# Attention with chunk selection, then a wave mixer: scores of two heads on halves of the TensorE array, the mask as a second product

## The chip, the cores and the metric

The kernel runs on one NeuronCore of a Trainium2 chip. The metric is the device time of one execution in microseconds (us). Three runs before the change took 250.59, 250.40 and 251.05 us, median 250.59. The profiled execution has a span of 250.7 us, from its first to its last instruction, with a mean granted TensorE clock of 0.986. All durations below come from that one execution.

## What is computed

The inputs q, k and v have 4 batches, 8 heads, 768 positions and 64 values a head (fp32). Keys fall into 24 chunks of 32. For every query a bound of its score against each chunk is formed from the chunk's minimum and maximum, the six best chunks that are not in the future are kept, and ordinary causal attention runs over the kept chunks alone:

```python
k_min, k_max = k_chunks.min(axis=3), k_chunks.max(axis=3)
ub = np.sum(np.maximum(q[..., None, :] * k_min, q[..., None, :] * k_max), axis=-1)
ub = np.where(causal, ub, -1e9)
top_chunks = np.argsort(ub, axis=-1)[..., -6:]
scores = np.where(sel & (pos[:, None] >= pos[None, :]), scale * q @ k.T, -1e9)
attn_out = softmax(scores) @ v
```

The 8 heads are put side by side to x (768 x 512 for each batch), and a mixer follows:

```python
theta = x @ w_theta
y = w_tok_r @ (x * cos(theta)) + w_tok_i @ (x * sin(theta))
u = x + y
out = u + np.maximum(u @ w_ch, 0)
```

## The kernel before, in words

The program is recorded first and emitted afterwards. `record` makes a list of operations. Each has a name, the engine (or several engines) that may run it, what it reads and what it writes. The long text `ORDER` gives the order of emission by the operations' numbers. A letter b or c behind a number takes the second or third engine of the choice. `F10` stands for ten filling products of 128 columns (L637), which keep TensorE (PE) busy and compute nothing. Ten more of 512 columns stand at the start (L633). Each engine runs its own instructions strictly in this order, so `ORDER` settles what stands behind what. `CLASSES` (L100) says how many buffers of each kind there are; `decode` (L654) hands them out in the order of use, and a buffer that is used again waits for its last reader.

For every batch b and every pair p of heads, `pair` (L188) does the following:

- It loads k and q of the two heads side by side (L174) and v (L182), all on SP's queue.
- It turns k and q with fp32 transposes on PE, three blocks at a time (L197), into `kps` and `qps`. Afterwards head 0 has partitions 0 to 63 and head 1 has 64 to 127.
- It copies k to `kx` and q to `qx` in fp16, each head by itself, to partitions 0 to 63 (L164 on ACT, L166 on DVE, L167 on POOL are the three choices of one copying helper). For the first two pairs of batch 0 (`direct`) k goes by way of an fp32 copy `kT`.
- It takes minimum and maximum over each chunk on DVE (L221, to `km`) and their difference (L226), and makes relu(q) as `qr` (L248 on DVE or POOL, L250 on ACT).

`group` (L258) makes the selection, in general for two pairs at once. The bounds `ub` are fp32 products of 64 rows by 32 columns (L280), placed by head on rows 0 or 64 of the array and by pair and run of queries on four column groups. Then DVE transposes them (L295), overwrites what lies in the future with a large negative value (L303), takes the eight largest of each query (L308), marks the chunks that fall below the sixth (L312) and transposes the marks to `nsT` (L317). From there the marks are copied into rows 64 to 87 of `qx`, by head, pair and run (L325). Rows 64 to 87 of the five `kx` buffers hold a one-hot of the key's chunk times -1000, loaded once by `Loh` (L531). Queries below 192 have at most six chunks and need no selection.

`head` (L335) forms one head's scores, transposed, so that keys are on partitions. One product over 88 rows (64 of k and q, 24 of one-hot and marks) gives score plus mask (L357). A head has three steps, each two key blocks: 1024, 1024 and 640 columns of PSUM, in two `sc` buffers of two banks each. In batch 0 the triangle on the diagonal is added by another product (L361). In the other batches it is cut after the exponential, on POOL (L377) or DVE (L375). ACT takes the exponential of a step to `pt` (L367). The weighted values `av` are 21 products of 65 columns with `pt` as weights (L398); the 65th column is the sum, by which DVE divides (L408, L409) into `x16`.

`mixer` (L413) turns x (L427), multiplies by w_theta (th, L437), takes sine and cosine on ACT (L444, L448), forms the products zr and zi (L452), multiplies by the turned token weights (y, L462 and L464), adds x (L470), turns the sum (ups, L478) and multiplies by w_ch (ch, L486); then come L492 and the store. PSUM buffers of class `mi` (three) serve all transposes, bounds and mixer products; `av` has one buffer.

Work of different batches overlaps: the list puts the next batch's pairs, selection and scores between the mixer products of the batch before.

Of the kernel before, what the change touches and what calls it, by code (L numbers as in the profile page):

```python
# [1 line left out]

# [8 lines left out]
FP16 = mybir.dt.float16  # L11
# [6 lines left out]
    "6 0 8 5 51 50 7 52 53 31 97 98 15 4 9 16 10 96 20 18 F10 54 12 13 60 11 14 55 95 26 61 17 19 22 56 27 64 "  # L18
    "76 23 62 58 30c 29 121 59 F19 67 28 24b 65 71 25 122 68b 72 57 70b 21 63c 75c F16 33 66 32 73b 120 34 69b "
    "74 42 F9 78 35 162 43 112 36 44 113 119 37 3 F11 110 45 87 111 117 46 38 F10 99 116c 49c 88 104 115 79 1 "  # L20
    "48b 100 89 41c 39b 108 47b 114 107 F17 228 226 101b 77 141 105 102 106 40c 227 103 406 90 F15 136 80 109b "
    "134 229 91 407 218 81 137 216 135b 219 168 163 217 F5 214 2 82 139c 123 140c 83 138 128 426 126 224 215 "
    "166 130b 86c 85c 132 125 222 84 221 94b 131 118 225 236 127 220 124b 164 133b 237 234 93 92 223 143 142b "
    "231 235 144 230 404 244 153 405 145 232 129 154 248 146 245 419 169 421 233 249 246 429 147 422 155 294 "
    "196 247 238 428 148 156 152b 427c 252 239 250 251 157 151c 184 295b 167 420b 276 253 160c 423b 278 193 "
    "425b 241 277 158 240 159 242 424 408 243 279 413 165 274 410 181 417 296 150c 161b 178 409b 275 264 412 "
    "197 411 265 284 416 198 437 285 418b 282 280 441 185 286 430 440 414 288 431 287 194c 281 187 283 202 438 "
    "266 195 289 182c 267 292 291 211 290 268 439 186 293 149b 179 432 269 254 434b 415 180 256 436 255 271 "
    "435 445 433b 257 272 442b 450 258 199 443 259 270 183 273 444 446 300 190 297b 260 448c 262 261 188 301b "
    "263 449b 447b 189 298 452 299 203 471 302 453 472 462 496 307 212c 304 463 495 454 312 464 455 451 309 "  # L30
    "213 308 306 311 313 322 310b 314 465 456 303 204 466 315 317 323 457 324 327 305b 208 318 468 461 474 470 "
    "332 459 319 467 316 333 328 473 458 339 321 329 469 544 325b 580 460c 545 480 331 340 330 484 341 483 334 "
    "482b 320 581 538 481b 475 539 191 342 479 497 557 326b 192 476b 335 558 577 478 582 541 477 174 540b 343 "
    "578 485 559 498 504 209c 344 542 508 546 205 551 579 345 210 336 200 506 549 488 552 507 543 583 337 201 "
    "489b 584 548 553 505b 547 499 338 585 486 172 501 550 564 176 487 175 554 170 500 586 491 492c 587 493 "
    "502 510 555 503 512 490 588 511b 753 346 513 509b 589 752 347 556 206b 567 516b 562 514b 754 560 515 519 "
    "207 568 561 529 348 565 520 569 349 530 521 350 531 755 177b 566 353 173b 522 374 517 354 171b 774 355 "
    "532 375b 523 778 356 533 357 524 537b 534c 358 563 494 526b 386 779 359 528c 570 536 776 527 642 525 571 "
    "535 635 387 351 777 643b 572 609 352 761 610 573 388 574 765 636 378 611 762b 603 379b 575 764 637 596 "
    "604 767 576 392 768b 763 605 606 597 393 644 607 769 598 394 645 590 822 518c 756 770 821 593 608 591 759 "  # L40
    "380 775 613 760 612 771b 376 381 798 632 592 757 766 395 772c 846 758 377b 793 396 594 614 841 389 615 "
    "773c 397 595 791 601 794 600 865 792 599 390 780 633 797b 785 845 783 622 360 788 796b 391 634 619 789 "
    "781 361 602 1102 787 362 623 782b 363 1103 364 784 786 624 620 365 795c 834 790b 366 629 799 835 367 630 "
    "621 800 1126 1127 368 631 801 640 810 638 639 802 842 382 811 803 616 646 617 641 1122 369 370 804 647b "
    "371 812 618 372 866b 805 626 813 836 809b 808 625 819 814 806c 627 837 915 807c 1169 383 816b 858 818 820 "
    "840c 628 817c 892 838 1170 398 916 859b 839 373 648 893 889 399 917 384 890 894 886 649 400 815c 860 385 "
    "655 887 861b 844 843 891b 670 863c 657 888 862 902 650 864b 656 905 659 897 672 1123 895 660 652 674 1101 "
    "896 658b 651 1100 654 662 665 653b 898 671 661 675 673b 667 664 663 680 666 681 676 401 668b 677 669 903 "
    "678 682 402 823 683 403 679 684 827 685 826 828 906 904 686 899 1125 825 912 832 1124 824 852 907b 900 "
    "831 687 688 855 833b 830 689 856 901 829 931 853 908 847 854 690 849 1168 1104 932 1167 848b 910 691 1105 "  # L50
    "850 925 1106 851 692 913 1108 909 694 693 926 695 933b 696 1107 1109 911 927 722 1110 1146 697 723 928 "
    "1112 990 1113 929 698 991 699 1114 1111b 918 930 734 700 919 914b 935 857 735 920 934 867 1147c 736 936 "
    "701 1193 877 868 702 1194 878 1117 869 879 724 1118 703 725b 870 704 1115 880 1141 871 1116 1189 705 881 "
    "1142 1121b 706 872 1120b 1133 937 883c 708 873b 882c 709 874b 1137 875c 876b 951 707 1134 944 1135 884 "
    "922 885 945 921 1136 923 710 952 924 946 957 1190 711 958 992 953b 954 1213 993 1119b 959 938 712 955 713 "
    "1128 939 714 956 962 941 1192 1132 960 1191 961 942 940 1131 967 963 726 1138b 1130 1139 943 970 1129 "
    "1140b 949 727b 948 947 1145 971 1184 1144 950 1148 1185 1143b 1214c 740 1158 972 968 1149 980 741 1182 "
    "981 969 983 1159 1150 742 737 1160 984 1151 964 1183 985 977 965 738 1188b 1176 715 739 1161 1187b 716 "
    "1179 966 975 1186 1162 974 978 973 1180 728 1166c 717 976 729b 979 718 1177 1165 719 1152 1178 1163 720 "
    "1153 730 1164 1157b 1154c 721 1171 731b 1253 1155c 1174 1250 1156c 1254 746 1175 1251 1172b 1234 1181 747 "  # L60
    "1173 1195 1237 1235 1252b 748 1199 743 982b 1198 1238 1240 1236b 986 744 988 1241 987 1239b 1260 745 989 "
    "1197 1247 1196 1208 1242b 1261 1255b 1244 1209b 1243 1245 1200 1248 1262 1246 1266 732 1206 1204 1267 "
    "1273 733 1207 1258 1268 1203 1279 1274 749 1212b 1202b 1210c 1201 994 750 1205b 1280 1276 996 1249b 1211b "
    "751 1281b 1263 997 1257 1277 1275b 1256 995 1215 1259 1264 998 1216 1278b 1271 1217 1008 1000 1265b 1218 "
    "1270 1225 1269 1219 1003 1272 1009 1220 1010 1282 1011 1283 1226 999 1284 1227 1023 1004 1001b 1005 1223 "
    "1013 1002 1024 1221 1007 1018 1025 1006b 1026b 1014 1027 1042 1019 1224 1043 1016b 1015 1285 1315 1312 "
    "1020 1021b 1340 1012 1313 1063 1228 1341 1017b 1064 1229 1065 1056 1232 1230 1066 1222 1022b 1316 1057 "
    "1058 1314b 1292 1317 1286 1293 1233c 1067 1231c 1287 1068 1294b 1299 1069 1044 1288 1300 1305 1045 1306 "
    "1046 1301 1047 1307 1302 1048 1289 1303 1049 1050 1290 1304b 1310 1318 1309 1319 1308 1291b 1051 1311 "
    "1052 1035 1320b 1322 1321 1323 1331 1324 1036 1332 1037 1295 1333b 1296 1297 1038 1298 1039 1040 1053 "  # L70
    "1041 1325 1054 1326 1342 1055 1328 1059 1343 1329 1060 1327b 1061 1330b 1076 1062 1072 1335 1073b 1336 "
    "1077 1334 1338 1337 1085 1339 1344 1086 1028 1345b 1029 1087 1074 1346 1075 1088 1348 1030 1089 1031 1032 "
    "1090 1347 1033 1350b 1078 1034 1366 1349 1079 1070 1368 1094 1071 1367 1370 1082 1095 1369 1080 1096 1083 "
    "1356 1081b 1084 1097 1358 1357 1351 1360b 1098 1091 1099 1353 1359b 1352 1371 1355 1092 1361 1354b 1373 "
    "1093 1372 1383 1375b 1363 1384 1385 1362 1374 1411 1412 1397 1364b 1398 1365b 1399 1413 1386 1414 1387 "
    "1388 1415 1389 1416 1400 1417 1376 1401 1428 1402 1429b 1377 1403 1420 1378 1421b 1379 1433 1380 1434 "
    "1381 1445 1435 1382 1390 1446 1404 1405 1447 1406 1407 1408 1409 1418 1410 1391 1419b 1392 1393 1430 1426 "
    "1431 1394 1427b 1395 1432 1424 1396 1442 1425b 1422 1443 1439 1423b 1444 1436 1440 1441 1437 1438 "
)

B, H, S, D = 4, 8, 768, 64
P = 128
DM = H * D
NT = S // P
CH = 32
NCH = S // CH
KX = D + NCH
QS = 192
NS = S - QS
RUN = NS // 2  # L90
NB = RUN // CH
SCALE = float(1.0 / np.sqrt(D))
NEG = -1000.0
# [615 lines left out]
```

The softmax here doesn't subtract the row's maximum and nothing guards it: scores larger than these inputs give would overflow.

## Time and profile before

| engine | busy us | share of the span |
|---|---|---|
| PE, products | 230.7 | 92% |
| PE, weight loads (beside products) | 139.0 | 55% |
| DVE | 186.3 | 74% |
| ACT | 184.2 | 73% |
| POOL | 101.5 | 40% |

| group of instructions | count | busy us |
|---|---|---|
| exponential, ACT L367 | 96 | 84.7 |
| scores, PE L357 | 256 | 52.2 |
| mixer y, PE L462 and L464 | 288 | 110.1 |
| chunk minimum and maximum, DVE L221 | 64 | 33.0 |
| weighted values, PE L398 | 672 | 30.2 |
| triangle after the exponential, POOL L377 | 47 | 20.0 |
| fp16 k from PSUM, ACT L164 | 40 | 18.7 |

The page of a profile gives busy time, a picture of the span in 40 slices, the chain of work that ended last, and groups of instructions by line with the mean time of one. Busy time of PE counts from the start of a product to its modelled end, so overlapping products hide small holes; the distance between the starts of two products shows them. The last instruction is the store of the last block of the output, after a last product ch at 246.5 us.

### The profile page before, as it was taken

To read this page: it belongs to the slowest core of one execution; us is meant where nothing else is said; L and a number is where in the kernel's file an instruction comes from. 1 tells how busy PE (TensorE), PEld (TensorE's weight loads), DVE (VectorE), ACT (ScalarE), POOL (GpSimd) and SP (SyncE) were. 2 spreads that over 40 slices of the span, in tenths; PEclk is the share of its full clock that TensorE was granted. 3 is DMA by queue.
4 is the path that set the end of the run, shared out by engine and by line. 5 is a ranking of instruction groups with operands and counts; after the bars stand their busy time and mean duration, and the time that the engine had idled before them with its cause. 6 is when DMAs were issued, how large, how long until landed. Compare 5 with 4: busy or idle time off the path is not lost.

```text
span 250.7 us, 5951 instructions
## 1 busy us (share of the span) xinstructions
PE 230.7 (92%) x2234; PEld 139.0 (55%) x2234; DVE 186.3 (74%) x563; ACT 184.2 (73%) x281; POOL 101.5 (40%) x172
## 2 busy tenths in 40 slices
PE   7989878779599999999999989999998999999993
PEld 2877666543257566666456557557653556444451
DVE  1889988459988598879697987999999357553433
ACT  2769999877769879969999289989996825571121
POOL 7755364163637543546631144560315100444000
PEclk9999999979889999999999999999999999999999
DMA  7999999999949999999523445112100000240114
GB/s 161 219 208 232 224 274 256 224 289 220 197 73 264 223 207 249 229 253 218 117 83 87 125 108 125 47 42 86 44 0 3 0 0 3 86 168 4 42 44 165
DMA packets 91154, 35.10 MB, mean 140 GB/s; under 512 B 85373, under 2 KB 85373, under 8 KB 91125
## 3 DMA queue, kind: packets, MB, share of 16 engines
q1 hardware_dynamic: 91124, 34.72, 63.1%
q8 instruction: 17, 0.28, 0.5%
q14 instruction: 13, 0.10, 0.1%
HBM read 26.06 MB, written 6.29 MB: 129 GB/s over the span
## 4 chain that ended last, share of the span: by engine, by line
PE 64%; DVE 14%; DMA 8%; ACT 5%; POOL 3%; issue 2%; SPq 2%; ACTq 0%
PE sc L357 11%; PE y L462 11%; PE y L464 11%; PE ch L486 7%; PE av L398 5%; DMA k<-in_k_dram 4%; PE ub L280 4%; DMA q<-in_q_dram 4%; PE qps L197 3%; PE kps L197 3%; DVE zr L452 3%; PE th L437 3%; DVE zi L452 2%; ACT pt L367 2%; POOL qr L248 2%
## 5 line engine op out<-in xcount | busy, mean ns | idle before, releaser
L367 ACT ACTIVATE pt<-sc 128x1024 f16<-128x1024 f32 (+1 forms) x96 | 84.7, 918 | 18.5 <-PE sc L357 14.8
L357 PE MATMUL sc<-qx,kx 88*128 88x512 f16 (+3 forms) x256 | 52.2, 307 | 5.4 <-DVE qx L325 3.3
L462 PE MATMUL y<-zr,wtokT 128*128 128x512 f16 x144 | 55.1, 382 | 1.3 <-DVE zr L452 1.1
L464 PE MATMUL y<-zi,wtokT 128*128 128x512 f16 x144 | 55.0, 382 | 0.0
L377 POOL TENSOR_SCALAR_AFFINE_SELECT pt<-pt 128x256 f16<-128x256 f16 x47 | 20.0, 427 | 47.5 <-ACT pt L367 47.1
L357 PEld LDWEIGHTS <-kx 88*128 88x128 f16 x256 | 23.3, 98 | 22.9 <-issue 7.1
L221 DVE TENSOR_REDUCE km<-kps 128x12 f32<-128x384 f32 x56 | 29.1, 548 | 5.2 <-PE kps L197 3.3
L398 PEld LDWEIGHTS <-pt 128*128 128x128 f16 x672 | 26.9, 98 | 9.2 <-DVE x L409 2.0
L398 PE MATMUL av<-v,pt 128*128 128x65 f16 x672 | 30.2, 194 | 1.9 <-ACT pt L367 1.1
L470 DVE TENSOR_TENSOR u<-y,x 128x512 f16<-128x512 f32 x24 | 16.5, 687 | 12.8 <-PE y L464 12.8
L437 PE MATMUL th<-wtheta,xT 128*128 128x512 f16 x96 | 23.7, 381 | 0.8 <-ACT sn L444 0.7
L486 PE MATMUL ch<-wch,uT 128*128 128x512 f16 x96 | 24.3, 379 | 0.0
L492 DVE SCALAR_TENSOR_TENSOR ot<-ch,u 128x512 f32<-128x512 f32 x24 | 16.5, 688 | 8.2 <-PE ch L486 8.0
L420 ACT COPY uT<-ups 128x512 f16<-128x512 f16 x15 | 8.8, 585 | 18.5 <-PE ups L478 18.3
L464 PEld LDWEIGHTS <-wtokT 128*128 128x128 f16 x144 | 14.1, 98 | 14.0 <-issue 2.7
L448 ACT ACTIVATE cs<-th,pi 128x512 f16<-128x512 f32 x24 | 16.6, 701 | 7.0 <-PE th L437 6.7
L462 PEld LDWEIGHTS <-wtokT 128*128 128x128 f16 x144 | 14.2, 98 | 13.2 <-issue 1.0
L164 ACT CAST kx<-kps 64x384 f16<-64x384 f32 x40 | 18.7, 473 | 1.7 <-PE kps L197 0.9
L409 DVE TENSOR_TENSOR x<-av,rec 128x384 f16<-128x384 f32 x32 | 17.8, 558 | 1.1
L452 POOL TENSOR_TENSOR zr<-x,cs 128x512 f16<-128x512 f16 x7 | 8.4, 1203 | 24.3 <-ACT cs L448 24.3
L197 PE MATMUL kps<-ident,k 128*128 128x128 f32 x96 | 15.6, 282 | 2.1 <-DMA k<-in_k_dram 1.2
L452 POOL TENSOR_TENSOR zi<-x,sn 128x512 f16<-128x512 f16 x9 | 11.2, 1250 | 14.1 <-ACT sn L444 14.1
(78 smaller groups left out, 389.2 us busy)
## 6 DMA issues: line engine op xcount, KB each, us to landing
k<-in_k_dram SPq DMA_DIRECT2D x32, 192.0 KB, 3.7
q<-in_q_dram SPq DMA_DIRECT2D x32, 192.0 KB, 4.5
v<-in_v_dram SPq DMA_DIRECT2D x16, 384.0 KB, 5.2
out_dram<-ot SPq DMA_DIRECT2D x24, 256.0 KB, 2.3
wtok<-in_moe_w_tok_r_dram SPq DMA_DIRECT2D x6, 384.0 KB, 6.4
wtok<-in_moe_w_tok_i_dram SPq DMA_DIRECT2D x6, 384.0 KB, 5.0
wth<-in_moe_w_theta_dram SPq DMA_DIRECT2D x4, 256.0 KB, 4.5
wch<-in_moe_w_ch_dram SPq DMA_DIRECT2D x4, 256.0 KB, 4.4
```

The source lines that it names most:

```text
L164: c = {"A": ("ACT", int(n * 0.833 + 60), 0, lambda: nc.scalar.copy(out=out(), in_=in_())), "D": ("DVE", int(n / 0.96 + 70) if psum else in ...
L197: nc.tensor.transpose(T(ps)[:, i * P:(i + 1) * P], T(src)[:, 3 * f + i, :, :].rearrange("p x d -> p (x d)"), K.ident32)
L221: nc.vector.tensor_reduce(out=T(km)[:, j, 12 * f:12 * f + 12], in_=src().rearrange("p (c w) -> p c w", w=CH), axis=AX.X, op=o)
L357: nc.tensor.matmul(T(ps)[:, a0:a1], T(kx)[0:KX, x, j * P:(j + 1) * P], T(qx)[0:KX, x, q0 + a0 - o:q0 + a1 - o], start=True, stop=True)
L367: nc.scalar.activation(out=T(pt)[:, BASE[s]:BASE[s] + w], in_=T(ps)[:, 0:w], func=AF.Exp, bias=0.0, scale=SCALE)
L377: eng.affine_select(out=a, in_=a, pattern=[[0, 2], [1, P]], compare_op=ALU.is_ge, fill=G.zero_reg(), base=0, channel_multiplier=-1)
L398: nc.tensor.matmul(ps[:, t, :], T(pt)[:, o:o + P], T(v16)[:, x, j, :], start=(j == 0), stop=(j == t))
L437: nc.tensor.matmul(T(ps), T(xT[c])[:, t * P:(t + 1) * P], K.wtheta[:, c, :], start=(c == 0), stop=(c == 3))
L452: eng.tensor_tensor(out=T(dst), in0=T(x16)[:, t, :], in1=T(src), op=ALU.mult)
L462: nc.tensor.matmul(T(ps), K.wtok[:, si, 0, t * P:(t + 1) * P], T(zr[si]), start=(si == 0), stop=False)
L464: nc.tensor.matmul(T(ps), K.wtok[:, si, 1, t * P:(t + 1) * P], T(zi[si]), start=False, stop=(si == NT - 1))
L486: nc.tensor.matmul(T(ps), T(uT[t])[:, c * P:(c + 1) * P], K.wch[:, c, :], start=(c == 0), stop=(c == 3))
```

## The change

Both heads of a pair stay on their own halves of the partitions throughout:

- k and q become fp16 in one copy for both heads (`kh`, `qh`), straight from PSUM for k and from the fp32 copy for q. The chunk minimum and maximum of k are always read from PSUM. The fp32 copy of k in the first two pairs is gone; those two transposes use an `sc` buffer. Making relu(q) on POOL is no longer among the choices.
- Scores of two heads are two 64-row products, at rows 0 and 64 of the array, into two PSUM banks. The mask is a second 64-row product into the same place, of a one-hot `ohr` (made on the chip by POOL) with `nsT` itself, for the queries from 192 up. The copies L325 and the one-hot loads L531 are gone.
- A pair has six steps (`STEPS`), each covering both heads, in place of three per head. The triangle is cut after the exponential in all batches.
- The selection is laid out per pair: `ub`, `ubT`, `ns` and `nsT` each hold one pair's two heads. In batch 0 every pair is selected by itself, and one extra bf16 product (`later`, loaded once) sets the future's bounds low. In other batches the second pair of a group comes out with its heads exchanged, so its last transpose is done in two pieces that put them back.
- Seven of the 32 `av` results are taken from the `mi` buffers.
- `ORDER` is new as a whole, and so is the place of nearly every load on SP's queue. It has 49 filling products of 128 columns in place of 112.

The core of the diff (`ORDER`, the helper for relu and the loading of v, which move, and the shapes of bounds are cut):

```diff
-SEGS = [(0, 4), (1, 3), (2, 5)]
+STEPS = [[(0, 0, 512)], [(0, 512, 256), (4, 512, 256)], [(1, 128, 512)], [(1, 640, 128), (3, 384, 384)],
+         [(2, 256, 512)], [(5, 640, 128)]]
...
-    "kx": (5, (2, S), FP16, "sb", True),
-    "qx": (5, (2, S), FP16, "sb", True),
+    "kh": (5, (S,), FP16, "sb", False),
+    "qh": (5, (S,), FP16, "sb", False),
-    "nsT": (3, (NB, 32), FP16, "sb", False),
+    "nsT": (5, (NB, 32), FP16, "sb", False),
-    "pt": (3, (2688,), FP16, "sb", False),
+    "pt": (3, (2, PW), FP16, "sb", False),
...
+            copies(f"evk.{b}.{p}.{f}", 384, 1, True, rd, [(kh, f)], lambda fs=fs: T(kh)[:, fs], src, "AD")
...
+            copies(f"cq.{b}.{p}.{f}", 384, 0, False, [(qT, f)], [(qh, f)],
+                   lambda fs=fs: T(qh)[:, fs], lambda fs=fs: T(qT)[:, fs], "PAD")
...
+            if first:
+                for y in range(n):
+                    nc.tensor.matmul(T(ub[y])[:, 0:run], K.later[:, 0:P], K.later[:, P:P + run], start=True, stop=False,
+                                     skip_group_check=True)
...
+                for x in range(2):
+                    nc.vector.transpose(flat(nsT)[x * D:(x + 1) * D], flat(ns)[(1 - x) * D:(2 - x) * D])
...
-                    def cp(eng, qx=qx, r=r, w0=w0, nsT=nsT, x=x):
-                        eng(out=T(qx)[D:KX, x, QS + r * run:QS + (r + 1) * run],
-                            in_=T(nsT).rearrange("p i c -> p (i c)")[w0:w0 + NCH, 0:run])
...
-                        nc.tensor.matmul(T(ps)[:, a0:a1], T(kx)[0:KX, x, j * P:(j + 1) * P],
-                                         T(qx)[0:KX, x, q0 + a0 - o:q0 + a1 - o], start=True, stop=True)
...
+                for j, q0, c in step:
+                    for x in range(2):
+                        h = slice(x * D, (x + 1) * D)
+                        nc.tensor.matmul(T(ps)[:, 512 * x + o:512 * x + o + c], T(kh)[h, j * P:(j + 1) * P],
+                                         T(qh)[h, q0:q0 + c], start=True, stop=False, skip_group_check=True)
+                    for r in range(2):
+                        a0, a1 = QS + r * NB * CH, QS + (r + 1) * NB * CH
+                        c0, c1 = max(q0, a0), min(q0 + c, a1)
+                        for x in range(2):
+                            h = slice(x * D, (x + 1) * D)
+                            if c0 < c1:
+                                nc.tensor.matmul(T(ps)[:, 512 * x + o + c0 - q0:512 * x + o + c1 - q0],
+                                                 K.ohr[h, r, j * P:(j + 1) * P],
+                                                 T(nsT).rearrange("p i c -> p (i c)")[h, c0 - a0:c1 - a0],
+                                                 start=False, stop=True, skip_group_check=True)
+                    o += c
...
-        av = buf("av", f"av.{b}.{h}")
+        av = buf("mi" if x and (b == 0 or p == 3) else "av", f"av.{b}.{h}")
...
-        op("SP", f"Loh.{i}", 350, [], [("oh", i)],
-           lambda i=i: nc.sync.dma_start(out=G.kept["kx", i][D:KX, :, :], in_=K.oh_h.ap()), dma=250)
+    op("SP", "Llater", 450, [], [("later", 0)], lambda: nc.sync.dma_start(out=K.later, in_=K.later_h.ap()), dma=350)
...
+                nc.gpsimd.affine_select(out=a, in_=a, pattern=[[-1, NCH], [0, CH]], compare_op=ALU.not_equal, fill=neg,
+                                        base=-(D * x + 32 * r), channel_multiplier=1)
```

The numbers in the recorded operations (350, 450 and the like) are what the order was planned with; nothing at run time reads them.

## The prediction

> **What bounds the kernel now.** I read the page's busy shares and its 40 slices first (each digit a tenth of a slice of 6.3 us), to see which engine is full and when.
>
> ```profile
> PE 230.7 (92%) x2234; PEld 139.0 (55%) x2234; DVE 186.3 (74%) x563; ACT 184.2 (73%) x281; POOL 101.5 (40%) x172
> PE   7989878779599999999999989999998999999993
> ```
> ```profile
> DVE  1889988459988598879697987999999357553433
> ACT  2769999877769879969999289989996825571121
> DMA  7999999999949999999523445112100000240114
> ```
>
> TensorE (PE) is at 9 in nearly every slice from the middle on, but not early, where ACT, DVE and the transfers are at 8 or 9. So I asked for windows cut where the work changes: batch 0's attention (8 to 53), its mixer's start (53 to 75), batches overlapped (75 to 188), the hand-over (188 to 200), the last mixer (200 to 238). Columns: length, then busy time and instructions of PE, weight loads, DVE, ACT, POOL, then clock, DMA share, GB/s.
>
> ```profile
> 8.00:53.00 45.00, 37.83 (x546) 29.46 (x545) 37.48 (x131) 40.44 (x66) 22.50 (x39) 1.00 1.17 238
> 53.00:75.00 22.00, 18.32 (x108) 8.82 (x109) 18.06 (x55) 14.84 (x22) 11.11 (x13) 0.84 0.97 183
> 75.00:188.00 113.00, 110.64 (x1156) 68.26 (x1154) 96.31 (x309) 100.20 (x156) 49.53 (x83) 1.00 0.62 139
> 188.00:200.00 12.00, 10.97 (x66) 5.32 (x65) 8.02 (x17) 8.98 (x11) 4.91 (x8) 1.00 0.01 1
> 200.00:238.00 38.00, 38.00 (x286) 20.11 (x283) 20.26 (x40) 15.25 (x23) 8.12 (x7) 1.00 0.13 50
> ```
>
> Up to 53 us ACT is fullest (40.4 of 45) and the DMA engines are full; PE's 37.8 holds some 8 us of filling products (the warm rows). From 75 us PE is busy 98% and more. Busy overstates a pipelined PE, so I added start-to-start times instead: 1024 columns of fp16 take 0.44 us (three score products in the chain of waits), 15 weighted-value products 0.47, six fp32 transposes 0.66. From 75 to 237.5 us that gives about 150 of 162.5: some 12 us of real gaps. From 75 us on, what is added to PE is mostly added to the end.
>
> The last view is the timeline around the bounds (ub, L280), the only products now on parts of the array: 64 rows by 32 columns.
>
> ```profile
> 157.10 0.27 PE L197 MATMUL qps<-ident,q 128*128 128x128 f32 x1
> 157.30 0.47 PE L280 MATMUL ub<-qr,km 64*32 64x288 f32 x8
> ```
> ```profile
> 158.09 0.41 PE L280 MATMUL ub<-qT,km 64*32 64x288 f32 x2
> 158.43 0.39 PE L486 MATMUL ch<-wch,uT 128*128 128x512 f16 x1
> ```
> ```profile
> 141.03 0.19 PE L398 MATMUL av<-v,pt 128*128 128x65 f16 x1
> 141.15 0.43 PE L280 MATMUL ub<-qr,km 64*32 64x288 f32 x2
> ```
>
> Two things are to be seen. Eight bounds, each 0.43 long, are over in 0.47: the two row halves and four column groups work at once. And at either end there is a hole. A transpose takes 0.11, but the first bound starts 0.20 after the last one: 0.09 lost. A weighted-value product takes 0.03, and the bound follows after 0.12: 0.09. The last ub starts at about 158.10 and streams 0.24 (the second eight start that much after the first), but L486 starts at 158.43: 0.09. Everywhere else products of different lines follow each other within 0.01. Cutting the array differently costs about **0.092 us, each way**.
>
> **What the Trainium skill says.** "TensorEngine Tiling (Array Packing)", section Tiling Modes: changing the tiling mode, not just the tile, drains TensorE, and 64x128 stands there as a mode of its own. It gives no price; the trace agrees for 64x32, with 0.092, and shows no 64x128. The same page, Restrictions and Gotchas: row halves must write to different PSUM banks; old and new bounds and the new scores do. "TensorE: Matmul & The Clock Gate", Part 3, says products of different row groups start about 4 ns apart; here eight start within 0.04 us, so it agrees roughly.
>
> **The change, part by part.**
>
> *Scores on PE.* Now a head's two 1024-column pieces and the 640 take 0.44 + 0.44 + 0.28, so a pair takes 2.32. New: keys by queries (2688 columns) and then one-hot by mask (2432 columns, only queries from 192 up), each once for both heads if the halves overlap: 5120 columns at 0.43 per 1024 = 2.15. The bounds took 1.13 - 0.09 = 1.04 for four rounds of 0.24, so 0.03 per change of round; a pair has 14 such changes in its six steps, taken at 0.02: 2.43. Twelve pairs of batches 1 to 3: 12 x 0.11 = **+1.3**. Batch 0 also drops 48 triangle products (2.7 us of PE), where PE isn't the bound: 0.
>
> *Changes of tiling.* Scores become half-array products, and the order scatters them between transposes, weighted values and mixer. In PE's instruction list of both programs I counted changes between full-array products, scores in halves and bounds: 18 before, 169 after. Batch 0's part, up to the first theta product: 7 and 42. That is 35 x 0.092 = 3.2, hidden by the filling products and the gaps up to 53 us: 0. Later: 11 and 127, so 116 x 0.092 = **+10.7**, with PE full. The trace has no row-only tiling, so the ends are 0 and 0.092; below nothing is excluded, since before has no such change to win back. I take the upper end, because the skill treats both as modes and both directions cost the same with different neighbours.
>
> *Copies, selection, ACT, DVE, POOL.* I priced each list of instructions by the rows of the groups. k: 64-partition pieces (ACT 0.47, DVE 0.55) become half as many of 128; q likewise (POOL 0.84 for 768 columns becomes 0.50 for 384, on all partitions); the 68 mask copies (0.20 to 0.43 each, 25 us over three engines) go, since the mask is multiplied from the transposed selection itself; relu leaves POOL (1.68 each) for ACT (0.69) and DVE (0.46); 24 triangles of batch 0 go to POOL (0.43) or DVE (0.30); every odd pair's second transpose has two pieces (6 x 0.46); two more ACT tables (1.28 each). Sums: ACT -18, POOL -35, DVE only -5. Up to batch 0's last normalisation ACT loses 9 but DVE 3, and DVE has only 7.5 us free in 45, so that stage ends 3 earlier: **-3** (0 to -8). Later the relief can only fill PE's 12 us of gaps; the named waits there are mostly PE on DVE, eased least. A third: **-4** (0 to -8).
>
> *Transfers and preparation.* Five one-hot loads (72 KB each, SP 0.4 to 0.5) become one of 106 KB, ahead of q's second piece of pair 1 and batch 0's v; 0.25 MB less at 238 GB/s is 1 us of a full DMA stage: 0 taken, -1 kept. The other loads move past each other on SP's queue, k of batch 1 behind two theta loads and one token weight; they bring the same bytes before batch 0's mixer: 0, with 2 either way. Preparing the one-hots puts four 768-column selects on POOL (0.29 for 128 columns, 0.41 for 256: about 0.9 each, an estimate), less 2.1 saved: POOL's start ends near 7.2 instead of 5.6, before its first copy is due (7.1 now, later after): 0.
>
> *Waits.* A pair's scores wait for one selection of both heads in place of copies by head; behind them on PE stand other pairs' transposes and values. Second heads' values use the shared PSUM buffers in seven pairs, so a transpose behind them may wait for a normalisation (0.75): 0 to +2, inside the range.
>
> Sum on its own span: 250.7 + 1.3 + 10.7 - 3 - 4 = **255.7**. The other runs shown are 250.4 to 251.05, median 250.59, as the span, so 255.6.
>
> **Rivals.**
>
> *Row halves switch freely.* If the hole belongs to column tiling alone, 116 changes cost 0 to 0.03: at most 3.5, say 1.7, and 250.7 + 1.3 + 1.7 - 3 - 4 = **246.7**, faster, 243 to 249. For it: no row-only change is in the trace. Against: the hole is equal on the way back to full columns. It decides below (3 + 4 - 1.3)/116 = 0.05 us per change, in the stage from 75 us.
>
> *The switches are paid, but relief is worth ACT's sum.* Batch 0 ends 8 earlier and gaps give back 7: 250.7 + 12 - 15 = **247.7**. For it: ACT is the fullest engine up to 53 us. Against: DVE is close behind and DMA full.
>
> *The halves don't overlap.* Then a pair takes 4.3: 12 x 2.0 = 24 on PE, plus the switches, less 7: **278**. Against: eight bounds in 0.47.
>
> **How the numbers follow.** Forecast 0.56, free switching 0.27, large relief 0.10, no overlap 0.04, other 0.03. The forecast's own range is 250 to 262; the whole range, 244 to 262, takes in the faster cases and leaves out no overlap and the tails. A measurement of this kernel tells about 0.3% (0.8 us) from no change. Faster: nearly all of free switching and large relief, and a tenth of the forecast's low end, 0.38; same 0.06; slower 0.56.
>
> **What would show it.** The timeline at the start and end of a block of scores: a hole of 0.09 (forecast) or none (rival). The group of scores: two products of 512 columns within 0.02 us of each other. Windows: PE at 98% from 75 us on, batch 0's first theta product (56.2 now) at about 53, and ACT's total 18 lower. The prediction is wrong if the holes are under 0.05, or if gaps on PE vanish while the holes are there.

## The result, and the profile after

The changed kernel takes 246.82 us (median of four runs, 246.31 to 247.59) beside 250.5 (249.75 to 251.05) for the one before: a ratio of 0.986, 95% interval 0.982 to 0.990. It is **faster by 1.4%**, where slower was forecast. Measured again beside eleven runs of the one before (after_again, below), it took 246.83 for 251.71, a ratio of 0.981 (0.977 to 0.985). The profiled execution has a span of 245.0 us; a run's time lies 1.7 above its span (246.73 here). The profiled execution of before took 252.39, 1.9 above the median of its runs, so the spans differ by 5.7 where the runs differ by 3.7.

First the page of after: busy shares, then the 40 slices of three engines and the transfers.

```profile
PE 232.7 (95%) x2495; PEld 130.6 (53%) x2495; DVE 179.5 (73%) x544; ACT 168.3 (69%) x242; POOL 68.9 (28%) x142
...
PE   7999899779999999999999999999899999999993
...
DVE  2899999789876986789939788938891449573364
ACT  2779989792787798689976994999789541580000
...
DMA  7999988999989599999221760111100001220024
```

ACT and POOL lost 16 and 33 us, DVE 7, about what the forecast counted (18, 35, 5). PE (TensorE) is at 9 in nearly every slice from the tenth on, and of the first ten slices six are at 9, where before had three. Its busy time went up by 2 us although the program got shorter. The chain of waits (each step of the end followed back to what released it) says the same by engine; before, PE held 64% of it, DVE 14% and DMA (the transfers) 8%.

```profile
PE 80%; DVE 10%; ACT 6%; DMA 2%; SPq 1%; issue 1%
```

The windows of after, at the cuts used for before (length, busy time and instructions of PE, weight loads, DVE, ACT, POOL, then clock, DMA share, GB/s):

```profile
8.00:53.00 45.00, 40.60 (x547) 26.02 (x546) 41.06 (x132) 39.13 (x60) 14.39 (x28) 1.00 1.02 245
53.00:75.00 22.00, 21.30 (x218) 11.04 (x224) 17.62 (x55) 15.13 (x24) 9.79 (x14) 1.00 1.07 241
75.00:188.00 113.00, 111.53 (x1304) 63.13 (x1289) 88.38 (x288) 93.43 (x133) 34.01 (x72) 1.00 0.51 122
188.00:200.00 12.00, 12.00 (x124) 6.08 (x121) 5.13 (x11) 7.22 (x8) 2.80 (x7) 1.00 0.01 1
200.00:238.00 38.00, 38.00 (x274) 19.61 (x274) 20.91 (x44) 10.85 (x17) 1.97 (x3) 1.00 0.15 55
```

In the first two windows PE does more than before (40.6 for 37.8, 21.3 for 18.3), and in the first DVE does too (41.1 for 37.5): the work of batch 0 and what follows it has moved forward. From 75 us on PE is busy 99%.

The forecast's first test was the hole at a block of half-array scores. This is the timeline of after around such a block (start, length, engine, line, shapes):

```profile
131.32 0.22 PE L464 MATMUL ups<-ident,u 128*128 128x128 f16 x1
131.47 0.39 PE L329 MATMUL sc<-qh,kh 64*128 64x512 f16 x2
...
132.16 0.28 PE L337 MATMUL sc<-nsT,ohr 64*128 64x288 f16 x2
132.38 0.39 PE L472 MATMUL ch<-wch,uT 128*128 128x512 f16 x1
```

A product of 128 fp16 columns streams in 0.055 (1024 in 0.44), but the first score starts 0.15 after the last `ups`: about 0.095 lost. At the end 288 columns stream in 0.12, and `ch` starts 0.22 later: 0.10 lost. The holes are there, at the forecast size. The halves overlap as well: two 512-column products are over in 0.39, where one takes 0.38.

So where is the gain? Busy time can't say, because a modelled end hides a hole of 0.1. I added up the starts instead: each product its streaming time, each change of the array's cut (full array, or parts of it) its hole, and what is left is PE without work.

| PE, us | before | after |
|---|---|---|
| full-array products except scores | 156.9 | 157.3 |
| scores and bounds | 49.2 | 46.6 |
| holes at changes of cut | 1.7 (18 changes) | 16.2 (171) |
| filling products | 8.3 | 4.8 |
| without work | 29.2 | 14.7 |

What is missing to the spans lies before the first product and after the last, 5.4 us in both. The holes cost 14.5 us more, and almost exactly that much time without work is gone. What is left is in the scores and in the filling products.

Part of the difference is a matter of the clock. In the profiled execution of before, the granted clock falls to half in two stretches of 3.4 us (the clock is the third number from the end), and products stream at half their pace there; the profiled execution of after has no such stretch inside its work.

```profile
53.30:56.70 3.40, 3.37 (x40) 1.56 (x41) 0.90 (x2) 1.40 (x2) 2.38 (x3) 0.50 1.25 298
66.90:70.30 3.40, 3.08 (x10) 1.60 (x10) 3.25 (x6) 1.02 (x1) 1.71 (x3) 0.50 0.67 164
```

A product y, for one, starts 0.43 after the last one at 69.5, and 0.22 after it at 70.6. Against the usual streaming times the two stretches lose 3.1 us: 1.0 in the bounds at 54.1 (32 products in 2.15, elsewhere 1.13), which the table counts with the scores, and 2.1 in other products, which it counts as without work. Beside after_again the mean clock of before was 0.983 to 0.999, that of after 0.992 to 1.0. What brings the stretches on, and whether the change makes them rarer, was not tested.

By time of day the difference falls into two parts. These are the last normalisations of batch 0 on DVE, in the timeline of before and then of after:

```profile
52.71 0.56 DVE L409 TENSOR_TENSOR x<-av,rec 128x384 f16<-128x384 f32 x1
```
```profile
43.59 0.56 DVE L395 TENSOR_TENSOR x<-av,rec 128x384 f16<-128x384 f32 x1
```

**Batch 0's attention ends 9.2 us earlier** (53.3 to 44.1), not 3. From there to the end of the span the changed kernel takes 3.5 us longer (200.9 for 197.4): holes +10.9, scores and bounds -1.4, other products +0.6, time without work -6.8 (14.8 to 8.0). The half-pace stretches are 1.0 of the 1.4 and 2.1 of the 6.8. The 9.2 are a lead at that one point: at the first y of batch 0 it is 6.3 (62.4 to 56.1), and at the end of the span 5.7.

### The profile page after: what moved, and what is told of

Its sections match the earlier page's. It is cut to its first block, busy times and chain, and to the rows that moved or that the text cites. A ratio compares the mean times of both kernels' runs of the same rounds, so it can differ in the third digit from the quotient of the medians.

```text
span 245.0 us, 6319 instructions
## 1 busy us (share of the span) xinstructions
PE 232.7 (95%) x2495; PEld 130.6 (53%) x2495; DVE 179.5 (73%) x544; ACT 168.3 (69%) x242; POOL 68.9 (28%) x142
## 4 chain that ended last, share of the span: by engine, by line
PE 80%; DVE 10%; ACT 6%; DMA 2%; SPq 1%; issue 1%
PE y L448 13%; PE y L450 12%; PE sc L329 10%; PE ch L472 9%; PE av L384 7%; PE sc L337 6%; PE th L423 5%; PE qps L215 4%; PE ub L265 4%; PE kps L215 4%; PE xps L413 2%; PE ups L464 2%; ACT pt L345 2%; DVE km L224 2%; DMA k<-in_k_dram 2%; DVE zr L438 1%
## 5 line engine op out<-in xcount | busy, mean ns | idle before, releaser
L345 ACT ACTIVATE pt<-sc 128x1024 f16<-128x1024 f32 (+1 forms) x96 | 85.2, 922 | 14.8 <-PE sc L337 14.0
L357 POOL TENSOR_SCALAR_AFFINE_SELECT pt<-pt 128x256 f16<-128x256 f16 x73 | 30.4, 418 | 103.6 <-ACT pt L345 102.9
L224 DVE TENSOR_REDUCE km<-kps 128x12 f32<-128x384 f32 x64 | 33.4, 550 | 7.7 <-ACT kh L160 4.7
L329 PE MATMUL sc<-qh,kh 64*128 64x512 f16 (+3 forms) x256 | 37.0, 309 | 1.1 <-ACT pt L345 1.0
L337 PE MATMUL sc<-nsT,ohr 64*128 64x288 f16 (+6 forms) x384 | 36.0, 247 | 0.2 <-DVE nsT L306 0.2
L384 PE MATMUL av<-v,pt 128*128 128x65 f16 x672 | 31.2, 194 | 0.8 <-DVE x L395 0.8
L337 PEld LDWEIGHTS <-ohr 64*128 64x128 f16 x384 | 19.0, 95 | 7.5 <-issue 0.5
L448 PEld LDWEIGHTS <-wtokT 128*128 128x128 f16 x144 | 14.0, 97 | 16.2 <-issue 2.9
L406 ACT COPY uT<-ups 128x512 f16<-128x512 f16 x10 | 5.8, 589 | 22.9 <-PE ups L464 22.9
L329 PEld LDWEIGHTS <-kh 64*128 64x128 f16 x256 | 12.3, 93 | 17.3 <-issue 14.5
L160 ACT CAST kh<-kps 128x384 f16<-128x384 f32 x23 | 10.9, 483 | 9.1 <-PE kps L215 8.1
```

Source lines behind the costliest of these rows:

```text
L224: nc.vector.tensor_reduce(out=T(km)[:, j, 12 * f:12 * f + 12], in_=src().rearrange("p (c w) -> p c w", w=CH), axis=AX.X, op=o)
L329: nc.tensor.matmul(T(ps)[:, 512 * x + o:512 * x + o + c], T(kh)[h, j * P:(j + 1) * P], T(qh)[h, q0:q0 + c], start=True, stop=False, skip_g ...
L337: nc.tensor.matmul(T(ps)[:, 512 * x + o + c0 - q0:512 * x + o + c1 - q0], K.ohr[h, r, j * P:(j + 1) * P], T(nsT).rearrange("p i c -> p (i ...
L345: nc.scalar.activation(out=T(pt)[:, :, base:base + w], in_=T(ps).rearrange("p (x c) -> p x c", x=2)[:, :, 0:w], func=AF.Exp, bias=0.0, sca ...
L357: eng.affine_select(out=a, in_=a, pattern=[[0, 2], [1, P]], compare_op=ALU.is_ge, fill=G.zero_reg(), base=0, channel_multiplier=-1)
L384: nc.tensor.matmul(ps[:, t, :], T(pt)[:, x, o:o + P], T(v16)[:, x, j, :], start=(j == 0), stop=(j == t))
```

## The experiments

Two theories stood against each other. In theory A, PE's own stream sets the time after the change: the drains are paid in it about one for one, and what outweighs them comes from the copies that are gone. In theory B, a good part of the holes lies where PE would have waited for the exponentials and their two score buffers anyway, so that removing changes of cut gives waits in return. Line numbers of the experiments are shifted by a few lines.

### The same columns without half arrays

```diff
-                    for x in range(2):
-                        h = slice(x * D, (x + 1) * D)
-                        nc.tensor.matmul(T(ps)[:, 512 * x + o:512 * x + o + c], T(kh)[h, j * P:(j + 1) * P],
-                                         T(qh)[h, q0:q0 + c], start=True, stop=False, skip_group_check=True)
+                    kj = T(kh)[:, j * P:(j + 1) * P]
+                    nc.tensor.matmul(T(ps)[:, o:o + c], kj, T(qh)[:, q0:q0 + c], start=True, stop=True)
+                    if q0 < QS:
+                        nc.tensor.matmul(T(ps)[:, 512 + o:512 + o + QS - q0], kj, T(qh)[:, q0:QS], start=True, stop=True)
...
-                                nc.tensor.matmul(T(ps)[:, 512 * x + o + c0 - q0:512 * x + o + c1 - q0],
-                                                 K.ohr[h, r, j * P:(j + 1) * P],
+                            nc.tensor.matmul(T(ps)[:, 512 + o + c0 - q0:512 + o + c1 - q0], K.ohr[:, r, j * P:(j + 1) * P],
```

> The scores as products of the full array: one product of both heads' k and q into the first PSUM bank, one of one-hot and marks (and of k and q for the queries below 192) into the second. The two heads are mixed and the mask is not added to a score, so this computes something else; PE streams 5376 columns a pair where the changed kernel streams 5120, and the exponentials, copies, selection and order are the same. Changes of tiling fall from 171 to 22, 149 fewer, 14.2 us of PE at 0.095, of which 10.3 lie after batch 0. Theory A (changes of tiling are paid on the path, as PE has hardly a gap left after batch 0): 246.8 - 10.3 + 1.2 = 237 to 239. Theory B (the changes cost PE time, but the other engines set the pace, so gaps come back in their place): 244 to 247.

It took 233.59 us (233.32 to 234.25), 0.929 of before (0.921 to 0.937); the span is 231.6, so **13.4 below after**. The busy line of its page, and the window from 75 to 188:

```profile
PE 219.8 (95%) x2207; PEld 137.0 (59%) x2207; DVE 175.2 (76%) x544; ACT 165.3 (71%) x242; POOL 69.5 (30%) x142
```
```profile
75.00:188.00 113.00, 112.55 (x1209) 72.57 (x1207) 87.95 (x283) 97.13 (x139) 36.96 (x76) 1.00 0.48 117
```

Scores and bounds stream 47.4 (46.6 in after), holes fall to 1.9 in 20 changes, and the time without work stays at 14.8. Holes -14.3 and scores +0.8 give -13.5, which is the measured difference. By parts it comes out less evenly. Batch 0 loses 3.4 us of holes and ends only 1.2 earlier (42.95 for 44.15): there they are mostly hidden. What follows is 12.2 shorter, where holes and scores account for 10.4 (-11.0 and +0.6); the rest is time without work. Theory A holds after batch 0: the drains are paid there, in full.

### More changes of cut

```diff
+                if b and s % 2 == 0:
+                    nc.tensor.matmul(T(ps)[:, 0:32], K.zero[0:D, 0:P], K.zero[0:D, 0:32], start=True, stop=True)
+                    nc.tensor.matmul(T(ps)[:, 0:32], K.zero[:, 0:P], K.zero[:, 0:32], start=True, stop=True)
```

> The changed kernel with two more changes of tiling ahead of every second step of scores in batches 1 to 3: a 64-row and a full product of 32 columns of zeros each, into columns that the step overwrites. 36 steps, 72 changes at 0.095 and 72 small products at about 0.025: 8.6 us more on PE. Theory A (PE sets the pace): 246.8 + 7 to 9 = 254 to 256. Theory B (others set it): 247 to 250.

It took 254.76 us (254.1 to 255.1), 8.0 more than after. The count of changes is 243, the holes are 23.0 (+6.8, so 0.094 for each of the 72 added), the added small products take 1.8, and the time without work is 15.1. So 8.6 us of additions on PE became 8.0 at the end. This is the forecast's price of 0.092, measured by itself.

### Scores grouped by two and by three

Both move only numbers in `ORDER`, so that two or three steps of scores stand together on PE; one place of each:

```diff
-78 193 79 98 96 184 194 375 185 97 199 376 80 180
+78 193 79 96 194 97 199 98 184 375 185 376 80 180
...
-348 492 445c 307 442 119 308 446 117 309 317
+348 492 445c 442 119 117 489 493 494 307 308 446 309 317
```

> The changed kernel with one thing moved: score steps that stood alone on PE are put next to the following step where at most three operations of PE stand between and inputs and buffers allow, in blocks of at most two; the order of every other engine is kept. Blocks of half-array products fall from 83 to 57, so 52 changes of tiling fewer, 4.9 us at 0.095. Theory A (PE sets the pace and every change is paid): 241 to 243. Theory B (a block of two steps has to wait for the exponential that frees its buffers, so the waits take the place of the changes): 246 to 250.

> The same, with up to eight operations of PE between and blocks of at most three or four steps: 45 blocks, 76 changes fewer, 7.2 us at 0.095. There are two score buffers, so a third step in a block waits for the first one's exponential (1.02 us against 0.45 for a step). Theory A: 239 to 242. Theory B: 246 to 252.

By two it took 249.72 us (249.53 to 250.36), by three 267.21 (266.28 to 269.19); after is 246.82. By two there are 119 changes for 171 and the holes fall by 4.9, but the time without work grows by 8.1. PE's waits (total us, times, longest) for a score buffer, in after, by two, and by three:

```profile
PE sc L329 <- ACT pt L345: 1.0, 2, 0.8
```
```profile
PE sc L328 <- ACT pt L344: 4.1, 8, 0.9
```
```profile
PE sc L328 <- ACT pt L344: 19.0, 22, 2.3
```

There are two `sc` buffers, and the exponential of a step takes 0.97 (two in a row show as 1.94 in the timeline of after). A second step can follow at once only if both buffers are free, a third never. Here theory B's mechanism holds: the scattering buys ACT's time, and its holes can't simply be grouped away. The two theories live side by side: holes are paid, but what stands between two steps is what lets ACT catch up.

### The copies back

In all batches, four 24-partition copies of the marks and the copies of k and q in two halves of 64 partitions are put back, inside the operations of the new order:

```diff
-                    lambda: nc.vector.tensor_copy(out=out(), in_=in_())),
+                    lambda: [nc.vector.tensor_copy(out=out()[a:z], in_=in_()[a:z]) for a, z in parts]),
...
+                    for i in range(4):
+                        eng = "DPADP"[(4 * (4 * b + p) + i) % 5]
+                        f = {"D": nc.vector.tensor_copy, "P": nc.gpsimd.tensor_copy, "A": nc.scalar.copy}[eng]
+                        f(out=T(nsM)[32 * i:32 * i + NCH], in_=T(nsT)[32 * i:32 * i + NCH])
...
-                                                 T(nsT).rearrange("p i c -> p (i c)")[h, c0 - a0:c1 - a0],
+                                                 T(nsM).rearrange("p i c -> p (i c)")[h, c0 - a0:c1 - a0],
```

> The changed kernel with the copying work of the kernel before put back, in the new order: k and q copied in two pieces of 64 partitions, and the marks copied in four pieces for a pair (24 rows of 288, on DVE, POOL and ACT in turn) just ahead of the pair's first scores. About 31 us of k and q copies and 24 us of mark copies over three engines. Theory R (relief of ACT, POOL and DVE is what ended batch 0 nine us earlier and closed PE's gaps): 254 to 260, batch 0's last normalisation back at 49 to 53, gaps back on PE. Theory O (the new order did it): 247 to 249.

It took 272.64 us (271.44 to 273.83), 25.8 more than after and far beyond what was expected. Its busy line:

```profile
PE 243.8 (90%) x2495; PEld 135.7 (50%) x2495; DVE 197.3 (73%) x591; ACT 190.5 (70%) x286; POOL 88.6 (33%) x184
```

PE has the same 2495 products and the same 171 changes of cut, so the 27.1 us by which its span is longer (272.1) are time without work, two half-pace stretches among them; batch 0 ends at 54.3. The 25.8 isn't what the change saved, though: the kernel before had such copies and only 29.2 us without work, in an order laid out around them, and these stand-ins load DVE with 18 us more, where before had 7 more. It shows that the copies reach PE, not how much they cost in before.

Then each kind by itself (the first of these two edits alone is `halves_back`, the other `marks_back`):

> The changed kernel with the copying of the marks alone put back: four copies of 24 rows by 288 for a pair, on DVE, POOL and ACT in turn, between the transposed selection and the pair's first scores. 64 copies of 0.33 to 0.43 us, 24 us over three engines. Theory R1 (the nine us in batch 0 come from the shorter way from selection to scores): first exponential 2 to 3 us later, batch 0's last normalisation at 49 to 53, total 254 to 262. Theory R2 (they come from fewer k and q copies): batch 0 at 45 to 47, total 248 to 252.

> The changed kernel with k and q copied in two pieces of 64 partitions again, all else as it is: 64 copies more of 0.43 to 0.55 us, 31 us over ACT (15), DVE (10) and POOL (6). Theory R1 (shorter way from selection to scores): batch 0's last normalisation at 45 to 47, total 248 to 252. Theory R2 (fewer k and q copies): at 49 to 53, total 254 to 262.

Marks alone: 260.99 us (260.02 to 261.41), batch 0's end +4.3, the span 13.9 longer. Halves alone: 261.57 (261.21 to 261.95), +4.4, and 14.2. Neither kind carries the loss: each gives about half, and 14.2 + 14.7 is near the 25.8 of both.

### The copies back in batch 0 alone

Both edits of the last section with `if b == 0`. This run was measured together with after_again, the changed kernel without an edit.

> The copying work put back (k and q in halves, marks in four pieces a pair) in batch 0 alone; batches 1 to 3 as in the changed kernel. Theory A (from batch 0's end on PE is full, so a late start is carried to the end): batch 0's last normalisation 10 later, at 53 to 55, and total 255 to 258. Theory C (later gaps take up the delay): 247 to 251.

> The changed kernel unaltered, beside the others of this call, for a narrower interval. Every theory: 246 to 248, ratio 0.983 to 0.989.

after_again took 246.83 us (246.72 to 248.28). back_first took 255.59 (253.49 to 256.26), **8.8 more**. The last normalisation of its batch 0 on DVE, and its window from 8 to 53:

```profile
52.79 0.56 DVE L403 TENSOR_TENSOR x<-av,rec 128x384 f16<-128x384 f32 x1
```
```profile
8.00:53.00 45.00, 37.26 (x516) 24.51 (x514) 37.83 (x127) 38.00 (x61) 17.46 (x41) 0.96 0.93 198
```

The line stands within 0.1 us of its place in before, and the window looks like that of before again (PE 37.3 for 37.8, DVE 37.8 for 37.5). The granted clock of 0.96 is one half-pace stretch, from 27.3 to 30.7; the one execution of back_first at a clock of 1.0 took 253.49, 6.7 more than after. Everything later is shifted by 9.2 to 9.5 and stays so to the end: the first y of batch 0 is at 65.3 (56.1 in after), that of batch 1 at 128.7 (119.4), that of batch 3 at 228.3 (219.1). So in the new order the copies of batch 0 cost some 7 to 9 us, and a late end of batch 0 is handed on one for one.

Where the start got shorter is seen at the first exponentials. First the timeline of before: a mark copy on POOL, a score on PE, the first exponential on ACT. Then after: the marks on DVE, the first score and the first exponential.

```profile
16.45 0.34 POOL L325 COPY qx<-nsT 24x192 f16<-24x192 f16 x1 [2.71 <-DVE nsT L317]
...
19.14 0.38 PE L357 MATMUL sc<-qx,kx 88*128 88x512 f16 x1
...
20.32 1.02 ACT L367 ACTIVATE pt<-sc 128x1024 f16<-128x1024 f32 x1
```
```profile
14.02 0.43 DVE L306 STREAM_TRANSPOSE nsT<-ns 128x288 f16<-128x288 f16 x1
...
14.29 0.23 PE L329 MATMUL sc<-qh,kh 64*128 64x128 f16 x2
...
14.78 0.38 ACT L345 ACTIVATE pt<-sc 128x256 f16<-128x256 f32 x1 [0.24 <-PE sc L337]
```

In before POOL waits 2.71 for the marks, copies follow on POOL and ACT until 18.99, and the first score starts at 19.14. In after the keys-by-queries product runs beside the transpose of the marks, and the mask product follows it. The first exponential comes 5.5 earlier; the other 3.7 come from batch 0's 24 exponentials in 26.6 us instead of 30.3. With the copies back in batch 0 the first came at 18.07, so 3.3 of the 5.5, and the 24 took 32.5, with the half-pace stretch among them.

So back_first meets the 9.2 of before by other parts, and that before lost its 9.2 to the copies isn't shown. A rival stands in its own chain of waits, where two transfers of 7 us each lead up to the end of batch 0:

```profile
29.73 7.02 DMA k<-in_k_dram
...
41.70 6.89 DMA q<-in_q_dram
...
48.72 0.52 PE qps L197 x3
...
51.35 1.22 DVE qx L166
...
52.71 0.57 DVE x L409
```

These are k and q of batch 1. `ORDER` of before put the transposes of this q ahead of the last scores of batch 0, and its copy on DVE just ahead of the last normalisation; PE waited 1.4 for the transfer. In the chain of after no transfer stands between 10 and 44 us. What the new order of loads and operations, with its fewer filling products, gives by itself wasn't measured.

### The old order with the new code

`ORDER` of before, its operations mapped to the new steps, with 51 moved back behind their inputs and buffers.

> The changed kernel's instructions in the order of the kernel before: every operation stands where the operation stood whose work it does, filling products too, moved back only where its inputs or a free buffer ask for it. Changes of tiling stay near 170. Theory R (relief): 246 to 250. Theory O (the new order): 254 to 262, with batch 0 ending near 53 and the gaps of before.

It took 286.3 us (283.41 to 287.32), with 49.6 us without work, slower than both kernels and than both expectations. Order and code are made for each other, so the gain can't be split into a part of each this way; the old code in the new order wasn't tried.

### No triangle

```diff
+                return
```

at the start of the cutting of triangles after the exponential.

> The changed kernel without the cut of the triangle after the exponential, so that future keys within a diagonal block count: 73 selects on POOL and 23 products on DVE less, some 37 us of their time, and the weighted values wait for the exponential alone. Theory A (in the changed kernel PE sets the pace and relief is used up): 243 to 246, what is gained lying in batch 0. Theory R (relief of the other engines still pays as it did in the change): 238 to 242.

It took 247.55 us (247.1 to 248.85), no gain. Its window from 75 to 188, where after had 34.01 on POOL:

```profile
75.00:188.00 113.00, 111.37 (x1299) 63.08 (x1281) 87.51 (x284) 93.23 (x133) 13.99 (x22) 1.00 0.50 122
```

PE's share is unchanged. The further gain hoped for isn't there, not in batch 0 either. There DVE loses 3.9 us of work, as the window from 8 to 44 shows (first after_again, then this run), and the last normalisation ends at 44.28, beside 44.15:

```profile
8.00:44.00 36.00, 33.75 (x510) 22.59 (x508) 33.65 (x116) 32.04 (x49) 12.38 (x25) 1.00 0.98 244
```
```profile
8.00:44.00 36.00, 33.83 (x512) 22.74 (x509) 29.76 (x101) 31.96 (x49) 9.15 (x16) 1.00 0.97 244
```

In after, this relief of DVE and POOL is worth nothing.

### Grouping where nothing is lost

Only the steps with a single PE operation between them are brought together:

```diff
-543 532 707 473b 548 540 721 708 533
+543 532 473b 548 540 707 721 708 533
```

> The gentlest grouping: after batch 0's attention, single score steps with exactly one operation of PE between them put side by side, nine times; 18 changes of tiling fewer, 1.7 us at 0.095, every other engine's order kept. Theory A (PE sets the pace): 244.5 to 246. Theory B, as the stronger groupings went (the second step waits for its buffer, and the operation pushed back is late for others): 247 to 249.

It took 245.94 us (245.69 to 246.59), 0.977 of before (0.971 to 0.982) and 0.9 below after_again, measured together with it (246.72 to 248.28). 153 changes for 171, holes 14.5, time without work 15.4. It beats both kernels, by about half of what was expected: of 1.7 us of holes 0.7 came back as waits.

## Why the prediction was wrong

- **Changes of tiling, +10.7: right.** The holes after batch 0 grew by 10.9 us, at 0.093 to 0.099 each. Full_array and more_changes show that they are paid. The rival in which the halves switch freely gave 246.7, within 0.2 us of the result, and is false: its number came by luck, by errors elsewhere.
- **Batch 0's own changes at nothing: nearly right.** In full_array 3.4 us of them are gone from batch 0, and it ends 1.2 earlier.
- **Batch 0 ends 3 earlier: the step that failed.** It ended 9.2 earlier (the first theta product is at 45.6, not near 53). The step took DVE's 3 us less of work as all that the stage can shrink, because DVE had only 7.5 free us of 45. But this idle time wasn't fixed: from 8 to 44 us after has 33.65 us of DVE work in 36, so about 2.4 idle. Nor does DVE's sum bound the stage: in no_triangle 3.9 us of it go and batch 0 ends no earlier. Copies bound it far more than their sum on DVE says: put back in the new order, they end batch 0 up to 9.2 later, and this reaches the end. How much of the 9.2 of before was the copies, and how much its order with the q of batch 1 ahead of the last scores, stays open.
- **Gaps give back 4: right in size, from a wrong reading.** Time without work after batch 0 fell by 6.8 of 14.8; without the half-pace stretches of before it is 4.7. The 12 us of gaps that were read between 75 and 237.5 come to about 9, when every product is counted by its streaming time. The copies experiments say that copies open such gaps (back_first to copies_back: 17 us more for batches 1 to 3); what share of the 4.7 is owed to the new order stays open.
- **Scores +1.3: wrong sign, small.** Scores and bounds after batch 0 took 1.4 less, 0.4 without the half-pace bounds. The 0.02 for each change of round came from fp32 bounds; with fp16 halves such a change measured between 0.001 and 0.015. The product count and the overlap were right.
- **Transfers, preparation and waits at nothing:** other products came to +0.6, and no new wait shows in after's list.

Put together, on the spans: 255.7, less 6.2 for batch 0, 3.1 for the half-pace stretches, 0.7 for gaps and 1.7 for scores, plus 0.6 for other products and 0.2 for holes: 244.8, beside 245.0. The clock is in no term of the forecast; about 2 of these 3.1 us aren't in the gain of 3.7, as the profiled execution of before was 1.9 above its median. The rival of large relief (247.7: batch 0 by 8, gaps by 7) came nearest in batch 0, and was turned down by the very argument on DVE. It took ACT's sum for the bound, which no run shows, and its 7 for gaps meets the 6.8 only with the clock's share in it.

## What to carry to other kernels

A half-full engine bounds a stage only if it would be busy to the end after the change: ask whether its idle time is a wait in the chain that the change shortens, and if so follow the chain of the first item through it, not the sums. Taking work off that engine alone tells whether it is the bound. Before two executions are compared term by term, compare the clock they were granted. Where PE sets the pace, count changes of array cut in the instruction list at 0.095 us each and take them at full price, but group half-array products only as far as the buffers they write are free. Two errors of opposite sign can land on a rival's number, so settle the mechanism in the timeline before believing the total.

## What was not expected of the hardware

- Cutting the array by rows only (64 by 128) costs the same 0.093 to 0.099 us each way as cutting it by columns too (0.092 from full to 64 by 32, and at the one change from 64 by 128 to 64 by 32). An 88-row product of before against a 128-row one costs 0.001 to 0.003. The Trainium skill, "TensorEngine Tiling (Array Packing)", section Tiling Modes, says that a change of mode drains TensorE; this case now shows a hole at such a change for 64 by 128 too.
- Within the half-array mode, scores and masks follow each other with at most 0.015 us lost, though rows and banks alternate: two products of 512 columns in 0.39 us. "TensorE: Matmul & The Clock Gate", Part 3, gives starts about 4 ns apart, which agrees with the 0.01 above one product's 0.38.
- In a stretch of 3.4 us with a granted clock of 0.50 each product streams at half pace: 512 columns in 0.43 us for 0.22. Four executions of after at a mean clock of 0.998 to 1.0 took 246.72 to 246.90 us, two at 0.992 took 248.23 and 248.28.
